# Cross-covariance attention followed by a multiplicative feed-forward layer: an earlier v load, quartered first folds, and a softmax chain issued one operation at a time

## The chip, the core and the metric

The kernel runs on one core of a Trainium2 chip. The core has a matmul engine (TensorE, "PE" in the profile, with its weight loads as "PEld"), a vector engine (VectorE, "DVE"), a scalar engine (ScalarE, "ACT"), a general-purpose engine (GpSimd, "POOL") and a queue engine (SyncE, "SP"). Each runs its own instructions in order and waits for the others by semaphores. Sixteen DMA engines move data for all of them. Matmul results go to PSUM, of which the kernel uses eight banks of 128 x 512 f32; everything else lies in SBUF. The metric is the device time of one execution in microseconds (us), taken as the median of several executions.

## What is computed

```python
def _attn_ref(q, k, v, tau):                                  # q, k, v: (4, 5824, 256)
    qn = q / (np.linalg.norm(q, axis=1, keepdims=True) + 1e-06)
    kn = k / (np.linalg.norm(k, axis=1, keepdims=True) + 1e-06)
    s = kn.transpose(0, 2, 1) @ qn / tau                      # (4, 256, 256)
    s = s - s.max(-1, keepdims=True)
    a = np.exp(s)
    a /= a.sum(-1, keepdims=True) + 1e-09
    return v @ a                                              # (4, 5824, 256)

def _moe_ref(x, w1, w2, w3, w_out):                           # x: (23296, 256)
    a = x @ w1                                                # w1, w2: (256, 1024)
    b = x @ w2
    h = a * b @ w3                                            # w3: (1024, 1024)
    return h @ w_out                                          # w_out: (1024, 256)
```

The attention matrix is only 256 x 256 for each of the four batches, since it is formed over the channels.

## The kernel before

**Algebra.** The attention matrix of a batch is folded into the weights: Wf = softmax x [w1, w2] (256 x 2048 for each batch), so that a and b come straight from v. Likewise W = w3 x w_out (1024 x 256) is formed once. Per batch there remain the scores G = q^T k with the norms of q's and k's columns, the softmax, the fold of w1 and w2, and the main work: a and b for all 5824 rows, their product, and the product times W.

**Main work.** `emit_ab(b, c, j)` (L423) makes one unit: batch b, chunk c of 512 rows (twelve chunks, the last of 192), column block j of eight. Four matmuls of 512 columns give a and b in two PSUM tiles of the tag "ab", which has four buffers; ScalarE casts a to bf16 ("as", L435), and VectorE multiplies it with b ("abs", L444). `emit_out` (L454), two units behind, multiplies the product with W into the PSUM tag "out" (three buffers); after eight units the result is copied by ScalarE and VectorE (L490, L491) and stored by SyncE. A buffer of a is free after its cast, a buffer of b after its product. The tag "G" (one buffer) holds the scores of the next batch.

**Order of the work.** The instructions are placed by hand (`manual_schedule`). While a batch's main work is emitted, `make_agenda(b)` (L604) lists other work for that time with due times, and `run_due` (L385) emits an item once a planned clock has passed its time. The clock counts the planned TensorE time of the emitted matmuls and a cost stated with each item. So an item stands at a place in every engine's queue that its due time sets; it isn't moved at run time.

**The items.** For batch n = b + 1: loads of q, k and v in pieces of eight rows a partition, each issued by GpSimd behind a tiny copy that waits for earlier work (L414 to L421); the 69 score units (`score_units`, L167) spread between t0 and t1; and the softmax (`soft_units`, L239) after t1:
- `norms` (L253): VectorE adds the two halves of the summed squares, and GpSimd sums them over all partitions.
- `k_row` (L262): 1/(sqrt(k's sum) + 1e-6) as four ScalarE operations in place, Ln, Exp, Ln, Exp, one directly behind the other (L271 to L274).
- `q_sums` and `q_norm` (L290, L293): VectorE takes q's sums from the diagonal, ScalarE takes Ln and Exp of them, VectorE adds 1e-6 and inverts.
- `scaled` (L316): two VectorE products of G with k's row (L306), then two ScalarE exponentials with q's factor as scale (L311), all four in one item.
- `sums` (L337): four matmuls with one column for the row sums, in a buffer of the tag "ab", and rs = 1/sum on VectorE.
- eight `fold`s (L359), each of two matmuls of 512 columns: fold i covers half i // 4 of the columns, w1 or w2 by i // 2 % 2, and 128 of the 256 rows by i % 2. Its result is evicted to Wf with the factor rs, by ScalarE for even i and by VectorE for odd i (L355, L357).

**The first batch.** Its scores and squares are matmuls that run as the pieces of q and k arrive (L540 to L578), with warm-up matmuls (`busy`, L205) in between. GpSimd issues the loads in the order of the code: k and q, then w1 and w2 in halves of 512 columns with the two halves of v's first piece between them, more of v, w_out and w3 (L552 to L563). After the scores come `scaled_first` and, behind four more warm-up matmuls, `first_folds` (L366): the row sums, folds 0 to 5, and between folds 2 and 3 eight transposes of v's first half piece on TensorE (`transpose_half_on_pe`, L138), whose copy to SBUF is VectorE's. Folds 6 and 7 are agenda items among the first units.

Of the kernel before, what the change touches and what calls it, by code (L numbers as in the profile page):

```python
# [15 lines left out]
P = 128  # L16
# [8 lines left out]
def kernel(  # L25
# [213 lines left out]
    def soft_units(n):  # L239
# [7 lines left out]
        def scaled_first():  # L247
            scale(0)
            q_norm(st["ss"])
            scale(1)  # L250
            exps()
# [10 lines left out]
        def k_row():  # L262
# [7 lines left out]
            kr = work.tile([P, C], F32, tag="kr", name=f"kr_{n}", bufs=1)  # L270
            nc.scalar.activation(out=kr, in_=src, func=AF.Ln)  # L271
            nc.scalar.activation(out=kr, in_=kr, func=AF.Exp, scale=0.5)
            nc.scalar.activation(out=kr, in_=kr, func=AF.Ln, bias=eps_t)  # L273
            nc.scalar.activation(out=kr, in_=kr, func=AF.Exp, scale=-1.0)  # L274
            st["kr"] = kr
# [14 lines left out]
        def q_sums():  # L290
            q_norm(diagonal(st["tot"][:, 0, :].rearrange("p (c t) -> p c t", t=P)))
# [16 lines left out]
        def exps():  # L308
            e = work.tile([P, CT, C], BF16, tag="e", name=f"e_{n}", bufs=2)
            for ct in range(CT):  # L310
                nc.scalar.activation(  # L311
                    out=e[:, ct, :], in_=st["s"][:, ct, :], func=AF.Exp, scale=st["r"][:, ct : ct + 1]
                )
            st["e"] = e

        def scaled():  # L316
            for ct in range(CT):
                scale(ct)
            exps()

        def sum_mm(c2):
            if c2 == 0:
                st["sum"] = psum.tile([P, 512], F32, tag="out" if n == 0 else "ab", name=f"sum_{n}", bufs=3 if n == 0 else 4)
                Wf[n] = wf_pool.tile([P, CT, 2, F], BF16, tag="Wf", name=f"Wf_{n}")
# [16 lines left out]
        def fold_mm(i, c2, tag="ab", on_act=None):  # L341
            h, rest = divmod(i, 4)
            w, c1 = divmod(rest, 2)
            if c2 == 0:
                st["fold", i] = psum.tile(
                    [P, 512], F32, tag=tag, name=f"fold_{n}_{i}", bufs={"ab": 4, "out": 3}[tag]
                )
            nc.tensor.matmul(  # L348
                st["fold", i], lhsT=st["e"][:, c2, c1 * P : (c1 + 1) * P], rhs=w12[:, c2, w, h * 512 : (h + 1) * 512],
                start=(c2 == 0), stop=(c2 == CT - 1),  # L350
            )
            if c2 == CT - 1:
                dst = Wf[n][:, c1, w, h * 512 : (h + 1) * 512]
                if on_act if on_act is not None else i % 2 == 0:
                    nc.scalar.activation(out=dst, in_=st["fold", i], func=AF.Copy, scale=st["rs"][:, c1 : c1 + 1])  # L355
                else:
                    nc.vector.tensor_scalar_mul(dst, st["fold", i], st["rs"][:, c1 : c1 + 1])  # L357

        def fold(i, tag="ab", on_act=None):  # L359
            fold_mm(i, 0, tag)  # L360
            fold_mm(i, 1, tag, i % 2 == 0 if on_act is None else on_act)

        def first_folds():
            sum_mm(0)
            fold_mm(0, 0)
            fold_mm(1, 0)  # L366
            sum_mm(1)
            fold_mm(0, 1)
            fold_mm(1, 1)
            fold(2)  # L370
            transpose_half_on_pe(0, 0, 0, False)
            fold(3, on_act=True)
            fold(4, "out", on_act=False)
            fold(5, "out")

        if n == 0:
            return [k_first, k_row, q_first, scaled_first, first_folds] + [lambda i=i: fold(i) for i in range(6, 8)]
        head = [(0.0, norms), (0.0, k_row), (0.0, q_sums)]
        return head + [(0.0, scaled), (0.2, sums)] + [(0.43, lambda i=i: fold(i)) for i in range(8)]


# [171 lines left out]
    for h in range(2):  # L553
# [150 lines left out]
```

## Time and profile before

| | |
|---|---|
| time, median of five executions | 574.86 us (574.6 to 576.18) |
| profiled execution, its own time | 574.86 us |
| profiled execution, span | 573.1 us |
| TensorE busy | 559.5 us, 98% of the span |
| TensorE weight loads busy | 355.5 us, 62% |
| VectorE busy | 377.2 us, 66% |
| ScalarE busy | 337.8 us, 59% |
| GpSimd busy | 83.2 us, 15% |
| granted TensorE clock, mean | 0.997 |

The page of the profile gives busy shares, then the span in 40 slices, the DMA queues, the chain of work that ended last, and the costliest groups of instructions. A group's line names line, engine, operation and tiles, the number of instructions, and after the bar the busy time, the mean length and the idle time before them with what ended it. Timelines give the start of a row, its length, and in square brackets the idle time in front of it. A matmul's length includes its way through the array, so rows of one engine overlap, and the busy share of TensorE is not a share of its peak. "Waits" names who waited for whom; where an instruction waits for several things, the one that came last is named.

### The profile page before, as it was taken

What the parts mean: (1) busy time and instruction counts of PE and PEld (TensorE: products, weight loads), DVE (VectorE), ACT (ScalarE), POOL (GpSimd) and SP (SyncE); (2) the same over time, 40 slices, a digit from 0 to 9 for tenths busy, and PEclk for the clock granted to TensorE, in tenths of its full rate; (3) what the DMA queues carried; (4) which work ended last, traced back from release to release, by engine and by line L of the source; (5) the groups of instructions that cost most, each with busy time, mean ns of one, the idle gap of its engine ahead of it and who ended that gap; (6) DMA issues with size and microseconds to landing.
All of it is one profiled execution on the core that took longest, in us unless ns stands there. A gap on an engine that the chain in (4) does not pass through costs nothing.

```text
span 573.1 us, 10096 instructions
## 1 busy us (share of the span) xinstructions
PE 559.5 (98%) x3744; PEld 355.5 (62%) x3750; DVE 377.2 (66%) x612; ACT 337.8 (59%) x624; POOL 83.2 (15%) x164
## 2 busy tenths in 40 slices
PE   7899999999999999999999999999999999999997
PEld 4765576776665666666656666666665666666665
DVE  1047744788877567887776567778876656565564
ACT  0046535777856567776756567767756554454453
POOL 5250020312030111211030012031120000000000
PEclk9899999999999999999999999999999999999999
DMA  8999959779665697395661595665740325221011
GB/s 165 211 189 209 197 99 231 180 160 231 132 174 120 127 204 148 88 195 118 144 147 59 108 218 118 138 138 121 181 110 38 85 73 148 63 62 75 38 70 59
DMA packets 74560, 76.93 MB, mean 134 GB/s; under 512 B 54160, under 2 KB 58256, under 8 KB 74512
## 3 DMA queue, kind: packets, MB, share of 16 engines
q0 software_dynamic: 15504, 39.46, 38.6%
q1 hardware_dynamic: 58784, 36.64, 22.1%
q8 instruction: 29, 0.48, 0.3%
q10 hardware_dynamic: 224, 0.20, 0.1%
q14 instruction: 19, 0.16, 0.1%
HBM read 78.91 MB, written 23.86 MB: 179 GB/s over the span
## 4 chain that ended last, share of the span: by engine, by line
PE 89%; ACT 4%; DMA 3%; DVE 2%; issue 1%; POOL 1%; ACTq 0%; DVEq 0%; POOLq 0%
PE o L470 26%; PE a L429 26%; PE b L429 26%; PE G L188 5%; DMA q<-in_q_dram 3%; PE fold L348 2%; ACT as L435 2%; DVE abs L444 1%; PE G L233 1%; PE w L587 1%; ACT e L311 1%; PE sqq L221 1%; PE sqk L221 0%; POOL k L109 0%; ACT kr L273 0%
## 5 line engine op out<-in xcount | busy, mean ns | idle before, releaser
L444 DVE TENSOR_TENSOR abs<-as,b 128x512 bf16<-128x512 bf16 x336 | 230.0, 686 | 140.9 <-ACT as L435 130.3
L435 ACT CAST as<-a 128x512 bf16<-128x512 f32 (+1 forms) x384 | 215.6, 563 | 178.8 <-DVE abs L444 92.1
L429 PEld LDWEIGHTS <-Wf 128*128 128x128 bf16 x1536 | 149.2, 98 | 102.6 <-issue 2.1
L429 PE MATMUL a<-vT,Wf 128*128 128x512 bf16 x704 | 209.4, 379 | 0.5 <-ACT as L435 0.5
L470 PE MATMUL o<-W_sb,abs 128*128 128x256 bf16 x1376 | 209.5, 273 | 0.1
L429 PE MATMUL b<-vT,Wf 128*128 128x512 bf16 x704 | 209.4, 379 | 0.0
L470 PEld LDWEIGHTS <-abs 128*128 128x128 bf16 x1376 | 134.4, 98 | 81.6 <-DVE abs L446 0.3
L197 DVE TENSOR_TENSOR acc<-acc,sq 128x1024 f32<-128x1024 f32 x66 | 80.5, 1219 | 0.2 <-ACT sq L185 0.2
L188 PE MATMUL G<-k,q 128*128 128x256 bf16 x276 | 49.8, 273 | 0.0
L185 ACT ACTIVATE sq<-q 128x512 f32<-128x512 bf16 x66 | 41.8, 633 | 0.0
L185 ACT ACTIVATE sq<-k 128x512 f32<-128x512 bf16 x66 | 41.6, 630 | 0.0
L417 POOL COPY gate_t<-abs 1x1 bf16<-1x1 bf16 x39 | 13.8, 354 | 170.0 <-DVE abs L444 169.3
L491 DVE COPY osb<-o 128x512 f32<-128x512 f32 x44 | 30.2, 686 | 0.7 <-PE o L470 0.7
L188 PEld LDWEIGHTS <-q 128*128 128x128 bf16 x276 | 27.0, 98 | 3.1
L421 POOL COPY gate_t<-vT 1x1 bf16<-1x1 bf16 x17 | 4.3, 254 | 168.9 <-DMA vT<-v 168.9
L490 ACT COPY osb<-o 128x512 f32<-128x512 f32 x44 | 25.8, 587 | 4.0 <-PE o L470 2.1
L271 ACT ACTIVATE kr<-row 128x256 f32<-128x256 f32 x1 | 0.4, 384 | 31.8 <-PE row L266 31.8
L109 POOL DMA_DIRECT2D q<-in_q_dram x29 | 15.6, 539 | 12.9 <-DMA k<-in_k_dram 5.6
L348 PE MATMUL fold<-w,e 128*128 128x512 bf16 x61 | 16.7, 379 | 0.3
L355 ACT ACTIVATE Wf<-fold,rs 128x512 bf16<-128x512 f32 x16 | 10.9, 687 | 7.9 <-PE fold L348 6.4
L244 DVE TENSOR_TENSOR dk<-sqk,ident 128x256 f32<-128x256 f32 x1 | 0.4, 425 | 21.7 <-PE sqk L221 21.7
L109 POOL DMA_DIRECT2D k<-in_k_dram x25 | 13.7, 548 | 3.7 <-DMA k<-in_k_dram 1.9
(90 smaller groups left out, 241.9 us busy)
## 6 DMA issues: line engine op xcount, KB each, us to landing
out_dram<-osb SPq DMA_DIRECT2D x44, 512.0 KB, 3.1
k<-in_k_dram POOLq DMA_DIRECT2D x19, 512.0 KB, 8.5
v<-in_v_dram POOLq DMA_DIRECT2D x19, 512.0 KB, 5.1
q<-in_q_dram POOLq DMA_DIRECT2D x18, 512.0 KB, 6.6
w_wout<-in_moe_w_dram POOLq DMA_DIRECT2D x1, 2048.0 KB, 23.1
k<-in_k_dram POOLq DMA_DIRECT2D x4, 320.0 KB, 9.9
v<-in_v_dram POOLq DMA_DIRECT2D x4, 320.0 KB, 5.3
q<-in_q_dram POOLq DMA_DIRECT2D x4, 256.0 KB, 11.9
```

What stands on the lines that cost most here:

```text
L109: nc.gpsimd.dma_start(out=pieces[nm, n, pi][:, lo:hi, :], in_=qk_main[nm, n][0][:, pi * PIECE + lo : pi * PIECE + hi, :])
L185: nc.scalar.activation(out=dst[:, :, part, :], in_=src[:, o : o + 2, :], func=AF.Square)
L188: nc.tensor.matmul(G[:, ct, :], lhsT=qt[:, i, ct * P : (ct + 1) * P], rhs=kt[:, i, :], start=(pr == 0 and part == 0 and ct == 0), stop=(pr ...
L197: nc.vector.tensor_add(accs[n], accs[n], sqs[0])
L348: nc.tensor.matmul(st["fold", i], lhsT=st["e"][:, c2, c1 * P : (c1 + 1) * P], rhs=w12[:, c2, w, h * 512 : (h + 1) * 512], start=(c2 == 0), ...
L417: nc.gpsimd.tensor_copy(gate_t, last_ab[0][:1, :1])
L429: nc.tensor.matmul(t[:, :n], lhsT=Wf[b][:, ct, w, j * P : (j + 1) * P], rhs=rhs_of(b, c, ct), start=(ct == 0), stop=(ct == CT - 1),)
L435: nc.scalar.copy(a_sb[:, :n], tiles[0][:, :n])
L444: nc.vector.tensor_mul(ab, a_sb, tiles[1])
L470: nc.tensor.matmul(tl[h][:, o, :], lhsT=lhsT, rhs=W_sb[:, j, :], start=(j == 0 and o == 0), stop=(j == FT - 1 and (small or o == 1)), skip ...
L490: nc.scalar.copy(o[:, 0:2, :], tl[0])
L491: nc.vector.tensor_copy(o[:, 2:4, :], tl[1])
```

## The change

Three things are changed together.

1. The first batch's loads: the first half of v's first piece is loaded ahead of w1 and w2, whose first 512 columns now come in two pieces of 256 each; the second halves of w1 and w2 follow in one piece each. The transposes of v's first half piece move from between the folds to the place between the warm-up matmuls (three instead of four) and the row sums.
2. The first batch's folds: the folds of the first 512 columns are made as eight results of 256 columns, in the order w1, w2, w1, w2; the first four use the tag "ab", the last four the tag "out". The folds of the other 512 columns, four of them, are agenda items among the first units.
3. The softmax of batches 1 to 3: each of the four k operations, q's sums, q's factor, each of the two products with k's row and each of the two exponentials is an agenda item of its own, 0.6 to 2.8 units of the clock apart. The row sums use the tag "G" in place of "ab". The folds are due later (from 18.0 in place of 15.5 after t1 + 1 and t1), 0.85 apart in place of 0.9. In the first batch's agenda t0 and t1 are 56 and 115 in place of 57 and 116.

```diff
@@ soft_units(n)
+        def k_step(i):
+            kr = st["kr"]
+            nc.scalar.activation(
+                out=kr, in_=kr if i else st["row"], func=(AF.Ln, AF.Exp)[i % 2],
+                scale=(1.0, 0.5, 1.0, -1.0)[i], bias=eps_t if i == 2 else 0.0,
+            )
...
         def q_sums():
-            q_norm(diagonal(st["tot"][:, 0, :].rearrange("p (c t) -> p c t", t=P)))
+            st["ss"] = diagonal(st["tot"][:, 0, :].rearrange("p (c t) -> p c t", t=P))
...
-        def scaled():
-            for ct in range(CT):
-                scale(ct)
-            exps()
+        def exps(ct):
+            if ct == 0:
+                st["e"] = work.tile([P, CT, C], BF16, tag="e", name=f"e_{n}", bufs=2)
+            nc.scalar.activation(
+                out=st["e"][:, ct, :], in_=st["s"][:, ct, :], func=AF.Exp, scale=st["r"][:, ct : ct + 1]
+            )
...
-                st["sum"] = psum.tile([P, 512], F32, tag="out" if n == 0 else "ab", name=f"sum_{n}", bufs=3 if n == 0 else 4)
+                st["sum"] = psum.tile([P, 512], F32, tag="out" if n == 0 else "G", name=f"sum_{n}", bufs=3 if n == 0 else 1)
...
         def first_folds():
             sum_mm(0)
-            fold_mm(0, 0)
-            fold_mm(1, 0)
+            for c1 in range(CT):
+                fold_mm((0, c1, 0, 256), 0)
             sum_mm(1)
-            fold_mm(0, 1)
-            fold_mm(1, 1)
-            fold(2)
-            transpose_half_on_pe(0, 0, 0, False)
-            fold(3, on_act=True)
-            fold(4, "out", on_act=False)
-            fold(5, "out")
+            for c1 in range(CT):
+                fold_mm((0, c1, 0, 256), 1, on_act=c1 == 0)
+            for w, lo in ((1, 0), (0, 256), (1, 256)):
+                for c1 in range(CT):
+                    for c2 in range(CT):
+                        fold_mm((w, c1, lo, lo + 256), c2, "ab" if lo == 0 else "out", c1 == 0)
 
         if n == 0:
-            return [k_first, k_row, q_first, scaled_first, first_folds] + [lambda i=i: fold(i) for i in range(6, 8)]
-        head = [(0.0, norms), (0.0, k_row), (0.0, q_sums)]
-        return head + [(0.0, scaled), (0.2, sums)] + [(0.43, lambda i=i: fold(i)) for i in range(8)]
+            return [k_first, k_row, q_first, scaled_first, first_folds] + [lambda i=i: fold(i) for i in range(4, 8)]
+
+        return (
+            [(0.0, 0.0, norms), (0.0, 7.5, k_row)]
+            + [(0.0, 7.5 + 1.3 * i, lambda i=i: k_step(i)) for i in range(4)]
+            + [(0.0, 8.0, q_sums), (0.0, 10.8, lambda: q_norm(st["ss"]))]
+            + [(0.0, 13.0 + 1.3 * ct, lambda ct=ct: scale(ct)) for ct in range(CT)]
+            + [(0.0, 13.6 + 1.3 * ct, lambda ct=ct: exps(ct)) for ct in range(CT)]
+            + [(0.2, 17.0, sums)]
+            + [(0.43, 18.0 + 0.85 * i, lambda i=i: fold(i)) for i in range(8)]
+        )
@@ loads and order of the first batch
-    for h in range(2):
-        hs = slice(h * F // 2, (h + 1) * F // 2)
-        nc.gpsimd.dma_start(out=w12[:, :, 0, hs], in_=w1r[:, :, hs])
-        nc.gpsimd.dma_start(out=w12[:, :, 1, hs], in_=w2r[:, :, hs])
-        if h == 0:
-            new_piece("v", 0, 0)
-        load_part("v", 0, 0, h * half, (h + 1) * half)
+    new_piece("v", 0, 0)
+    load_part("v", 0, 0, 0, half)
+    for f0, f1 in ((0, 256), (256, 512), (512, F)):
+        nc.gpsimd.dma_start(out=w12[:, :, 0, f0:f1], in_=w1r[:, :, f0:f1])
+        nc.gpsimd.dma_start(out=w12[:, :, 1, f0:f1], in_=w2r[:, :, f0:f1])
+    load_part("v", 0, 0, half, PIECE)
...
     soft0[3]()
-    busy(4)
+    busy(3)
+    transpose_half_on_pe(0, 0, 0, False)
     soft0[4]()
@@ make_agenda(b)
-            for i in range(2):
-                at(1.5 + 0.6 * i, 0.43, soft0[5 + i])
+            for i in range(4):
+                at(0.8 + 0.6 * i, 0.43, soft0[5 + i])
...
-            t0, t1 = 57.0, 116.0
+            t0, t1 = 56.0, 115.0
...
-        late = 2.5 if b == 0 else 0.0
-        ts = [t1 + 1.0] + [t1 + late + t for t in (8.5, 9.0, 11.0, 14.5)] + [t1 + late + 15.5 + 0.9 * i for i in range(8)]
-        for t, (cst, fn) in zip(ts, soft):
-            at(t, cst, fn)
+        for i, (cst, t, fn) in enumerate(soft):
+            at(t1 + 1.0 + t + (2.0 if b == 0 and i > 0 else 0.0), cst, fn)
```

## The prediction

> **What bounds the kernel now.** I read the page's chain first, then the waits of TensorE, then the timelines of single engines where TensorE stops, then the transfers of the first 45 us. The chain that ended last:
>
> ```profile
> PE 89%; ACT 4%; DMA 3%; DVE 2%; issue 1%; POOL 1%; ACTq 0%; DVEq 0%; POOLq 0%
> ```
>
> TensorE sets the time: a microsecond is won only where it stops, and its matmul work is the same before and after (64 fold matmuls, eight of them cut in two; one 0.22 us warm-up less, which lies in idle time). It stops at two kinds of place that the change touches. The first is the turn from scores to the first chunk (timeline of TensorE, then of ScalarE; columns are start, length, engine, line, operation, idle before it):
>
> ```profile
> 34.95 1.03 PE L209 MATMUL warm_I-482_483<-warm 128*128 128x512 bf16 x3
> 36.98 0.20 PE L327 MATMUL sum<-ones_b,e 128*128 128x1 bf16 x2 [1.00 <-ACT e L311]
> ...
> 37.53 1.02 PE L348 MATMUL fold<-w,e 128*128 128x512 bf16 x4
> 38.39 0.61 PE L132 MATMUL tr_I-511_512<-ident_b,v 128*128 128x128 bf16 x8
> 38.83 1.46 PE L348 MATMUL fold<-w,e 128*128 128x512 bf16 x6
> 40.13 0.59 PE L429 MATMUL a<-vT,Wf 128*128 128x512 bf16 x2
> ```
> ```profile
> 36.42 0.91 ACT L311 ACTIVATE e<-s,r 128x256 bf16<-128x256 f32 x2 [0.44 <-DVE r L298]
> 38.16 2.00 ACT L355 ACTIVATE Wf<-fold,rs 128x512 bf16<-128x512 f32 x3 [0.83 <-PE fold L348]
> ```
>
> TensorE waits for e until 36.98 and then runs without a gap to the first a at 40.13: 3.15 us, 0.44 of it (38.39 to 38.83) the transposes of v. Matmuls are spaced 0.217 us (512 columns), 0.109 (256), 0.083 (192) and 0.055 (128); a row's length adds a pipeline tail. The second kind of place is the softmax of a later batch. Batch 3, TensorE, then ScalarE:
>
> ```profile
> 434.45 0.60 PE L470 MATMUL o<-W_sb,abs 128*128 128x256 bf16 x4
> 435.87 0.24 PE L327 MATMUL sum<-ones_b,e 128*128 128x1 bf16 x4 [0.82 <-ACT as L435]
> 436.36 0.59 PE L429 MATMUL a<-vT,Wf 128*128 128x512 bf16 x2 [0.25 <-ACT as L435]
> ```
> ```profile
> 432.54 0.60 ACT L490 COPY osb<-o 128x512 f32<-128x512 f32 x1
> 434.44 0.91 ACT L311 ACTIVATE e<-s,r 128x256 bf16<-128x256 f32 x2 [1.31 <-DVE s L306]
> 435.25 1.05 ACT L435 CAST as<-a 128x512 bf16<-128x512 f32 x2
> ```
>
> The reader should see that ScalarE sits 1.31 us in front of its exponentials and that two casts lie behind them; "sum" takes one of the four a/b buffers and so waits for the first of those casts, not for e (ready at 435.35). By spacing, TensorE loses 435.87-434.45-0.44 = 0.98 and 436.36-435.87-0.10 = 0.39: 1.37 us. Batch 2 shows the same steps at 300.46, 301.88 and 302.37: 1.37. Batch 1 stops at the last chunk's start:
>
> ```profile
> 172.45 0.60 PE L470 MATMUL o<-W_sb,abs 128*128 128x256 bf16 x4
> 173.28 0.32 PE L429 MATMUL a<-vTt,Wf 128*128 128x192 bf16 x2 [0.23 <-ACT as L435]
> 173.76 0.33 PE L429 MATMUL b<-vTt,Wf 128*128 128x192 bf16 x2 [0.16 <-ACT as L435]
> 174.00 0.61 PE L470 MATMUL o<-W_sb,abs 128*128 128x256 bf16 x4
> ```
>
> That is 0.39+0.31+0.08 = 0.78, and further on gaps of 0.03 to 0.30 before folds and a/b of the short chunk (174.5 to 182.3), 0.9 in all.
>
> **The change, part by part.**
>
> *First stage, loads.* Each answer below is for one issue, at 29.85, 31.64 and 32.18 us in this order; the last column is microseconds to landing:
>
> ```profile
> w<-in_moe_w_dram POOLq DMA_DIRECT2D x1, 256.0 KB, 4.6
> v<-in_v_dram POOLq DMA_DIRECT2D x1, 256.0 KB, 5.6
> w<-in_moe_w_dram POOLq DMA_DIRECT2D x1, 256.0 KB, 7.0
> ```
>
> The last one lands at 39.18, where a weight load for fold 4 indeed waits for w until 39.18. v's first half now takes the place of the first w1 piece, so it lands near 34.5 (29.85+4.6); its eight transposes, placed behind three warm-up matmuls (34.95+0.65 = 35.6), run in the wait for e: -0.44 on the path. Their copy on VectorE (0.69, L136) fits between the second scale (ends 36.70) and rs (37.70). The w pieces follow: neighbours of 256 KB landed 1.2 to 1.9 us apart (34.45, then 30.56+5.2 = 35.76, 37.24, 39.18), so a quarter of 128 KB costs at least 0.6 and, if a piece cost the same whatever its size, at most 1.9; I take 0.9, because rows of half the length lower the rate (163 GB/s at 550 packets in 30 to 32 us, 219 at 123 packets in 20 to 22). The fourth quarter then lands at 34.6+3.6 = 38.2; TensorE reaches it at 38.6. The halves land near 39.7 and 41.1, wanted at 40.6 and 42.4; v's second half and piece 1 about 42.5 and 45.3, wanted at 44.2 and 47. GpSimd issues two DMAs more (0.72 each); behind them w3 is issued later, but it landed 23.1 us after issue, so the transfers are its limit, and its transposes (landed 63.1) had 3.4 us before the first w matmul at 66.50.
>
> Behind these spacings stands a rule that speaks against small pieces: the Trainium skill (DMA: Bandwidth & Descriptors, "Anatomy of one DMA — SWDGE (gpsimd) path") gives a DMA about 2.0 us fixed plus the bytes at 436 GB/s, which as an estimate makes 2.3 us a quarter; paid one after another, the fourth would land at 43.8 and the sum be some 5 us worse. Pieces of twice the size landing 1.2 to 1.9 us apart say that it is not paid in series.
>
> *First stage, folds.* In the built program's order folds 0 to 3 stand ahead of the first a as eight 256-column quarters, and folds 4 to 7 between the first a/b units (before: 0 to 5 ahead, 6 and 7 between). Four quarters use the "ab" buffers and four the three "out" buffers, so the eighth waits until ScalarE has evicted the fifth, and behind it the whole of TensorE's queue. ScalarE starts evicting at 38.16 (rs as before) and takes the first, third and fifth quarter in turn; a 128x256 ScalarE instruction with a scale vector costs 0.455 (e: 0.91 for two): the fifth is out at 38.16+3x0.455 = 39.53. TensorE is at the eighth by 38.83 (second sum at 37.47 as before, then 12 more matmuls), so it waits 0.7, ends it at 39.75 and has 2x0.433 = 0.87 us of folds more to come than before at 40.13. Net 39.75+0.87-40.13 = +0.49, say **+0.45**. From below: no wait, only the moved transposes, -0.44. From above: late pieces (rival D), +3.4.
>
> *Scores of batch 1.* With t0 at 56 and two folds more behind the first a, the score units stand up to 1.3 us earlier in TensorE's work; the first matmul on piece 4 of k 0.44 earlier. That one had little room: k's piece, issued at 128.01, landed after 10.2 at 138.2; its first G matmul started at 138.63. The gates in front of the load stand where they stood. 0 to +0.8, nearest to **+0.15**.
>
> *Softmax of batches 1 to 3.* The four kr steps, 0.42 to 0.51 each, now go singly between casts, before each of which ScalarE idled 0.71: they cost nothing as long as that idle time stands (else 0.4 a step). "sum" takes the G buffer, free once the second scale has read it, so it no longer takes an a/b buffer or waits for a cast. What stays is a round trip: in batches 2 and 3 the order is cast, product, scale, exponential, next cast. One round is 0.60+0.42+0.47+0.59 = 2.1 against 1.30 for a unit of TensorE; two rounds put ScalarE 1.6 behind, and a cast may lag about 1.3 (a's buffer is wanted again 2.17 after a ends; the cast itself takes 0.59, its start 0.2). A stall of about 0.35 is left, in front of a of the unit 10_7: -1.0 per batch. In exchange five or six folds move from full units, where they ran without gaps, into the short chunk, where batch 1 lost 0.9 with seven: +0.3 each, bounds 0 and 0.9. In batch 1 each exponential stands a cast later than its scale, so no round trip: -0.78; its folds start two units later, three at the end together: -0.2, bounds -0.9 and 0. Sum -1.0-0.7-0.7 = **-2.4**; bounds -4.4 (all stops gone: 0.78+0.9+2x1.37) and +1.5 (no slack in the rounds, 1.6+0.9-1.37 in two batches, -0.78 in the first).
>
> Casts between Ln and Exp cost no switch of tables: in the block of batch 3 a cast follows Exp at 435.25 with no idle time. The skill (ScalarE: Activation LUTs, "Table sets: the hidden batching unit") asks that calls be grouped by table set; at its 2.7 us a switch, a switch at every one of the eight split operations would make the sum some 20 us worse a batch.
>
> **Sum.** +0.45+0.15-2.4 = -1.8. The profiled execution took 574.86 us (span 573.1, 1.76 around it), the median itself, so 574.86-1.8 = 573.06: **573.1 us**.
>
> **Rivals.** B: the round trip eats batches 2 and 3; only batch 1 gains: 574.86+0.6-1.0 = 574.5. For it: the 1.31 us that ScalarE waits for scales today; against it: the buffers' slack. C: ScalarE evicts 256 columns in 0.37 (L480's copy) or the eighth quarter isn't held: start 0 to -0.44, 572.2. D, the other side: quarters land 1.9 us apart. The fourth is there at 42.2, 3.6 late, 0.7 of it covered: start +0.45+2.9, and the halves behind it another 0.7; 574.86+4.05+0.15-2.4 = 576.7. It passes the old time from about 1.45 us a quarter and the bound of what can be told from 1.75. Against it: two of the three spacings above are under 1.5 at twice the bytes. E, the change doesn't do what it says: v's half lands only at 37.24 as today, the transposes hold up the sums until 37.7: +0.7, 573.8.
>
> **How the numbers follow.** Likeliest case 0.60 (571.9 to 573.9: start -0.1 to +1, softmax -3 to -1.5), B 0.15, C 0.12, D 0.08, E 0.05. The range 571.9 to 575.2 leaves out D and the lower part of C. About 0.2% (1.15 us) is what can be told from no change. Faster, below 573.7: 0.54 of the likeliest, C, part of E: 0.67. Slower, above 576.0: D and a little: 0.09. Between: 0.24.
>
> **What would show it.** The v transposes in TensorE's timeline before the sums; the eighth quarter waiting for ScalarE near 38.8 to 39.5 and the first a near 39.7; no wait of "sum" on a cast, but one of some 0.3 of a on a cast in batches 2 and 3. Wrong if TensorE waits for w or v before 45 us, for k near 138 us, or if the short chunks lose more than 0.9 each.

## The result and the profile after

| | before | after |
|---|---|---|
| median | 574.97 us (62 executions, 574.6 to 576.72) | 575.71 us (36 executions, 573.95 to 579.84) |
| ratio | | 1.002, 95% interval 1.0012 to 1.0029 |
| profiled execution, its own time | 574.86 us | 574.51 us |
| profiled execution, span | 573.1 us | 572.4 us |

So the kernel became slower by 0.2%, where 573.1 us was forecast. The scatter says more than the median: before, all executions lie within 2.1 us, after they reach over 5.9 us, and thirteen of the 36 lie above 577. (Beside runs 9 to 12 two of 23 executions of the kernel before took 577.45 and 580.08 us: a single high execution shows nothing, thirteen of 36 do.) The one that was profiled took 574.51, 0.35 us less than the profiled one before. It still shows what went wrong. The chain of work that ended last, by engine and by line:

```profile
PE 85%; DMA 12%; POOL 1%; issue 1%; DVE 1%; ACT 1%; POOLq 0%; ACTq 0%; DVEq 0%
PE a L440 26%; PE b L440 26%; PE o L481 25%; DMA k<-in_k_dram 8%; PE G L188 4%; PE fold L350 2%; DMA v<-in_v_dram 2%; PE w L598 1%; DMA w<-in_moe_w_dram 1%; DMA vT<-v 1%; ACT as L446 0%; POOL q L109 0%; POOL k L109 0%; DVE abs L455 0%; POOL w L568 0%
```

DMA stood at 3% and is now at 12%, 8% of it loads of k. TensorE's timeline shows the place (start, length, engine, line, operation, idle before it with its releaser):

```profile
116.79 0.38 PE L188 MATMUL G<-k,q 128*128 128x256 bf16 x2 [0.20 <-DMA k<-in_k_dram]
...
137.64 0.60 PE L481 MATMUL o<-W_sb,abs 128*128 128x256 bf16 x4
139.19 0.60 PE L188 MATMUL G<-k,q 128*128 128x256 bf16 x4 [0.95 <-DMA k<-in_k_dram]
```

The brackets count idle time only; by spacing of the matmuls (139.19-137.64-0.44 = 1.11, and 0.36 at 116.79) TensorE loses **1.47 us** in front of scores of batch 1, because pieces 2 and 4 of k come late. Before, it lost nothing there:

```profile
138.19 0.60 PE L470 MATMUL o<-W_sb,abs 128*128 128x256 bf16 x4
138.63 0.60 PE L188 MATMUL G<-k,q 128*128 128x256 bf16 x4
```

The other two places changed in the way that was planned, the start at a higher cost. The start, TensorE:

```profile
35.24 0.61 PE L132 MATMUL tr_I-491_492<-ident_b,v 128*128 128x128 bf16 x8
36.62 0.20 PE L328 MATMUL sum<-ones_b,e 128*128 128x1 bf16 x2 [0.77 <-ACT e L318]
...
39.19 0.59 PE L440 MATMUL a<-vT,Wf 128*128 128x512 bf16 x2
...
40.44 0.59 PE L350 MATMUL fold<-w,e 128*128 128x512 bf16 x2 [0.23 <-DMA w<-in_moe_w_dram]
```

The transposes of v run in the wait for e, and the first a stands 2.57 us behind the first sum (before 3.15); with two folds more still to come, the fifth unit of a and b begins 8.66 us behind the sum (45.28-36.62), before 7.91 (44.89-36.98): +0.75 at equal work. And the softmax of batch 3:

```profile
438.19 0.60 PE L481 MATMUL o<-W_sb,abs 128*128 128x256 bf16 x4
438.62 0.24 PE L328 MATMUL sum<-ones_b,e 128*128 128x1 bf16 x4
438.88 0.59 PE L440 MATMUL a<-vT,Wf 128*128 128x512 bf16 x2
```

"sum" follows o without a wait (0.98 before); 0.16 and 0.06 are left in front of a and b, and some tenths between the folds that follow.

The account of the two profiled executions closes: the first sum 0.36 us earlier (in the execution before, the granted clock was one half from 21.20 to 24.61 us, among the scores of batch 0, and in this one it was not; for loads this one waited 0.5 us longer), start +0.75, k +1.47, and from the fifth unit to the last matmul 523.36 instead of 524.41, that is -1.05 with the 1.47 in it, so -2.52 for the softmax of three batches. Together -0.66; the spans differ by -0.67. (The time around the span was 2.1 instead of 1.8 us; why isn't known.)

**Why k is late.** GpSimd's timeline, before and then after: one-element copies to gate_t are the gates, which wait for the work named behind the arrow, and the DMA_DIRECT2D rows are the issues of loads.

```profile
72.22 0.18 POOL L421 COPY gate_t<-vT 1x1 bf16<-1x1 bf16 x1 [34.71 <-DMA vT<-v]
...
81.84 0.18 POOL L421 COPY gate_t<-vT 1x1 bf16<-1x1 bf16 x1 [8.25 <-DMA vT<-v]
...
126.76 0.18 POOL L421 COPY gate_t<-vTt 1x1 bf16<-1x1 bf16 x1 [13.97 <-DVE acc L197]
128.01 0.54 POOL L109 DMA_DIRECT2D k<-in_k_dram  x1
```
```profile
73.79 0.18 POOL L432 COPY gate_t<-vT 1x1 bf16<-1x1 bf16 x1 [34.72 <-DMA vT<-v]
...
85.01 0.18 POOL L432 COPY gate_t<-vT 1x1 bf16<-1x1 bf16 x1 [9.86 <-DMA vT<-v]
...
127.56 1.04 POOL L432 COPY gate_t<-vTt 1x1 bf16<-1x1 bf16 x1 [14.79 <-DVE abs L455]
129.67 0.54 POOL L109 DMA_DIRECT2D k<-in_k_dram  x1
```

Read downwards this is one chain: a transpose of v by SyncE's DMA lands, the gate opens, the next piece of v is loaded, is transposed, opens the next gate, behind which q and k are loaded, and so on. It begins with w3: SyncE transposes w3 in four steps ahead of v's third piece, and w3 landed at 60.41 instead of 59.14 (issue 37.57 with 22.8 us to landing; before 36.03 with 23.1). So the first gate opens 1.57 us later, the second 3.17, the last 0.80. In front of the last one the piece of v is issued when it was before (111.68, before 111.71), but lands 0.79 us later, behind the loads of q and k that the gates made late. The bracket of the last gate names VectorE; the transpose that it reads landed at 127.43 (before 126.64), 0.13 us (0.12) ahead of the copy, so it is this landing that opens the gate. There the copy itself takes 1.04 instead of 0.18, and the k load that lands at 139.14 is issued 1.66 us later than its counterpart, which landed at 138.19. TensorE wanted it at 138.63 before and at 138.08 now. The slow copy coincides with a sum of squares on VectorE, which before had just ended (before, then after):

```profile
125.44 1.22 DVE L197 TENSOR_TENSOR acc<-acc,sq 128x1024 f32<-128x1024 f32 x1
```
```profile
127.34 1.22 DVE L197 TENSOR_TENSOR acc<-acc,sq 128x1024 f32<-128x1024 f32 x1
```

The copy of 127.56 ends 0.04 us after this sum. So of the 1.66 us, 0.80 is the chain and 0.86 what the gate met by being late.

w3 itself is late because the loads ahead of it took longer (v's second half landed at 42.97, before at 41.69). Two windows of the first stage, before and then after (length, busy time of the engines with counts, granted clock, share of the DMA engines, GB/s):

```profile
35.50:37.50 2.00, 0.99 (x7) 0.29 (x6) 0.99 (x4) 1.35 (x5) 1.86 (x3) 1.00 1.03 168
```
```profile
35.50:37.50 2.00, 1.23 (x17) 0.79 (x15) 1.61 (x7) 1.03 (x3) 2.00 (x4) 1.00 0.97 127
```

The DMA engines are about as busy as before, but move 127 instead of 168 GB/s. A quarter's rows are 512 bytes, those of a half 1024, those of v 2048; the window before holds 163 packets of 1024 bytes and 83 of 2048, the one after 227 of 512 and 134 of 1024, so the order of the loads has its share in the difference. With the same order and halves (run 6 below) the window holds 302 packets of 1024 and none of the others:

```profile
35.50:37.50 2.00, 0.81 (x13) 0.40 (x10) 1.88 (x5) 1.08 (x3) 1.86 (x3) 1.00 1.10 155
```

A packet of 512 bytes took 61 ns in the mean of 28 to 60 us, one of 1024 between 104 and 108. By these times the quarters cost the sixteen engines 0.75 us more, of the 1.27 by which w3 is late; the rest is not accounted for.

The second gate lost more than the first, since the transposes in front of it took 5.3 us to land instead of 3.6. From the transfers while they run, before (78 to 82 us) and then after (79.5 to 85 us): an issue with its microseconds to landing, and a queue with its packets, MB and share of the engines:

```profile
vT<-v SPq DMA_TRANSPOSE x1, 3.6
```
```profile
q8 instruction: 1, 0.02, 1.1%
...
vT<-v SPq DMA_TRANSPOSE x1, 5.3
```

The transposes move 2080 packets in both; but after, one instruction fetch of 16 KB falls before the landing. In the packets of the trace all but two of the transposes' have started by 82.88; the fetch runs from 82.90 to 83.86, and the last two follow at 83.84 and 83.85. Before, the last ones moved at 81.25 and the fetch came at 83.16.

### The profile page after: what moved, and what is told of

It reads as the page before. It is cut to its first block, busy times and chain, and to the rows that moved or that the text cites. A ratio compares the mean times of both kernels' runs of the same rounds, so it can differ in the third digit from the quotient of the medians.

```text
span 572.4 us, 10114 instructions
## 1 busy us (share of the span) xinstructions
PE 558.8 (98%) x3751; PEld 355.1 (62%) x3757; DVE 377.3 (66%) x614; ACT 337.6 (59%) x626; POOL 85.8 (15%) x166
## 4 chain that ended last, share of the span: by engine, by line
PE 85%; DMA 12%; POOL 1%; issue 1%; DVE 1%; ACT 1%; POOLq 0%; ACTq 0%; DVEq 0%
PE a L440 26%; PE b L440 26%; PE o L481 25%; DMA k<-in_k_dram 8%; PE G L188 4%; PE fold L350 2%; DMA v<-in_v_dram 2%; PE w L598 1%; DMA w<-in_moe_w_dram 1%; DMA vT<-v 1%; ACT as L446 0%; POOL q L109 0%; POOL k L109 0%; DVE abs L455 0%; POOL w L568 0%
## 5 line engine op out<-in xcount | busy, mean ns | idle before, releaser
L197 DVE TENSOR_TENSOR acc<-acc,sq 128x1024 f32<-128x1024 f32 x66 | 80.5, 1219 | 0.7 <-ACT sq L185 0.7
L350 PE MATMUL fold<-w,e 128*128 128x512 bf16 (+1 forms) x69 | 16.6, 354 | 1.3 <-ACT Wf L357 0.6
L357 ACT ACTIVATE Wf<-fold,rs 128x512 bf16<-128x512 f32 (+1 forms) x18 | 11.3, 640 | 7.7 <-PE fold L350 7.3
## 6 DMA issues: line engine op xcount, KB each, us to landing
w_wout<-in_moe_w_dram POOLq DMA_DIRECT2D x1, 2048.0 KB, 22.8
```

Of the source, the lines that this page charges most:

```text
L197: nc.vector.tensor_add(accs[n], accs[n], sqs[0])
L350: nc.tensor.matmul(m, lhsT=st["e"][:, c2, c1 * P : (c1 + 1) * P], rhs=w12[:, c2, w, lo:hi], start=(c2 == 0), stop=(c2 == CT - 1),)
```

## The experiments

Three explanations stood at the start: K (k comes late), F (the first stage loses by late w or v) and S (the split softmax does). The first four runs split the change.

**1. Scores at their old place.**

```diff
-            t0, t1 = 56.0, 115.0
+            t0, t1 = 57.0, 116.0
```

> The changed kernel with t0 and t1 of the first batch back at 57 and 116; nothing else. Theory K (k comes late): in the profile of the changed kernel TensorE waits 0.36 us at 116.79 and 1.11 us at 139.19 for pieces of k, because w3's load lands at 60.41 (before: 59.14) and everything queued behind it, down to the k load issued at 129.67 (before: 128.01), is later, while the scores stand about 1 us earlier. With the scores about 0.9 to 1.0 us later the two waits shrink to about 0.1 to 0.3 in all, the profile shows that, the median falls by 1.2 to about 574.5, and the executions of 577 to 580 become rare. Theory F (the first stage makes the slow executions, by w or v coming late): no change, 575.7, with a third of the executions still above 577. Theory S (the split softmax does): no change either.

Measured: 576.4 us (574.08 to 579.53, 12 executions), ratio 1.0025 (1.0009 to 1.0041). The wait did not shrink, it grew:

```profile
141.20 0.38 PE L188 MATMUL G<-k,q 128*128 128x256 bf16 x2 [3.48 <-DMA k<-in_k_dram]
```

This k load was issued at 129.49, as in the changed kernel (129.67), but landed at 141.16 instead of 139.14; a store of the output was issued at 131.78 beside it, in the changed kernel only at 133.35. So theory K is right about the wait and wrong about its cure: one unit of the clock is less than the scatter of that load, which landed at 139.14, 140.76 (run 12) and 141.16 in the three profiles with this first stage and the split softmax.

**2. The split softmax alone.** Loads, folds and transposes of batch 0 as before, t0 and t1 at 57 and 116; of the change only the new agenda of `soft_units` and the row sums in "G". Against the changed kernel:

```diff
-    new_piece("v", 0, 0)
-    load_part("v", 0, 0, 0, half)
-    for f0, f1 in ((0, 256), (256, 512), (512, F)):
+    for h in range(2):
+        hs = slice(h * F // 2, (h + 1) * F // 2)
...
-    busy(3)
-    transpose_half_on_pe(0, 0, 0, False)
+    busy(4)
     soft0[4]()
...
-            t0, t1 = 56.0, 115.0
+            t0, t1 = 57.0, 116.0
```

> The split softmax alone: loads, folds and transposes of the first batch as before, t0 and t1 at 57 and 116. Theory K: no wait for k, and the softmax gains what the trace of the changed kernel shows when its waits are taken out (about 1.2 in batch 1 and 0.67 in each of batches 2 and 3, 2.5 in all): 574.97 - 2.5 = 572.5, executions close together as those of the kernel before. Theory F: the same 572.5. Theory S (the split softmax makes the spread, and gains little): 575 to 576, with executions above 577.

Measured: 573.6 us (573.53 to 573.86), ratio 0.9973 (0.9962 to 0.9983). No wait for k, and no scatter: theory S falls. The gain is 1.5, not 2.5: the last three chunks of a batch take 30.59, 29.90 and 29.74 us here (before 30.87, 30.78, 30.23), which is -0.28 in batch 1 and -0.88 and -0.49 in the others; 0.33 is lost again in the first stage, 0.32 of it to a wait for w at 39.68. In batch 1 the gain does not hang on t1 alone: in run 1, also with t1 at 116, the three chunks took 29.54 us, a gain of 1.1 at equal work (two matmuls of the scores, 0.22 us, lie ahead of them there). The planned clock of run 1 counts two folds more among the first units, 0.86 in all, and so emits what follows earlier; no run changed that alone.

**3. The first stage alone.** The changed kernel's loads, quarter folds and transposes, the old softmax, t0 and t1 at 57 and 116. Against the changed kernel:

```diff
+        def scaled():
+            for ct in range(CT):
+                scale(ct)
+            for ct in range(CT):
+                exps(ct)
...
+        head = [(0.0, norms), (0.0, whole_row), (0.0, whole_q)]
+        return head + [(0.0, scaled), (0.2, sums)] + [(0.43, lambda i=i: fold(i)) for i in range(8)]
...
-            t0, t1 = 56.0, 115.0
+            t0, t1 = 57.0, 116.0
```

> The first stage alone: v's half piece first, w1 and w2 in six loads, quarter folds, transposes ahead of the row sums; the softmax in its old form and t0 and t1 at 57 and 116. Theory K: the stage's own cost is the 0.75 us that the changed kernel is behind at equal work at 45 us, counted from the row sums, and the late k load costs 0.1 to 0.5 more with the scores at their old place: 574.97 + 0.75 + 0.3 = 576.0, few executions above 577.5. Theory F: it holds all of the loss and the spread: 575.7 + 2.5 = 578, a third of the executions above 579. Theory S: 575.0 to 575.7, close together.

Measured: 581.8 us (577.07 to 582.27), ratio 1.0091 (1.0063 to 1.0118). Far above what K expected, and not for w or v either. TensorE, and then a window of it:

```profile
141.18 0.59 PE L188 MATMUL G<-k,q 128*128 128x256 bf16 x2 [2.94 <-DMA k<-in_k_dram]
141.56 1.06 PE L447 MATMUL a<-vT,Wf 128*128 128x512 bf16 x2
```
```profile
142.00:146.00 4.00, 4.00 (x23) 2.37 (x22) 2.35 (x3) 2.26 (x5) 0.00 (x0) 0.77 1.02 200
```

Behind a wait of 3.10 us by spacing the matmuls stand 0.43 us apart instead of 0.216 until 143.9 (two of them take 1.06 instead of 0.59): the granted clock is one half, 0.77 in the mean of the window, its column behind the counts. From 141.18 on that costs 1.3 us more. Of its 6.5 us over the span before, 0.64 is the start, 3.26 the waits for k (0.16 of it at 118) and 1.3 the clock; the other 1.3 lie mostly in the old softmax of batch 1, which the folds moved behind the first unit put at another place (next run).

**4. The kernel before with early scores.**

```diff
-            t0, t1 = 57.0, 116.0
+            t0, t1 = 56.0, 115.0
```

> The kernel before with t0 and t1 at 56 and 115; nothing else. Theory K: the k piece that lands at 138.19 had 0.44 us to spare; with the scores about 1 us earlier TensorE waits some 0.5 us for it: 575.4 to 575.6, and the profile shows the wait near 138. It lacks the late w3, so its executions scatter less than those of the changed kernel. Theories F and S: 575.0, no wait for k.

Measured: 577.2 us (576.84 to 577.77), ratio 1.0035 (1.0023 to 1.0047), above what any theory gave. The wait for k is there as expected (0.56 by spacing, at 138.15). The larger part is another: with the earlier t1 the old softmax falls into full chunks.

```profile
171.48 0.59 PE L429 MATMUL a<-vT,Wf 128*128 128x512 bf16 x2 [0.22 <-ACT as L435]
...
173.95 0.59 PE L429 MATMUL a<-vT,Wf 128*128 128x512 bf16 x2 [0.71 <-ACT as L435]
```

With a b between them, TensorE loses 0.38, 0.29 and 0.88 by spacing. So the shift of t1 is bad for the old softmax; the split one, in the changed kernel, does not lose by it.

What the four leave: k is late wherever the new first stage is in, with either softmax and either place of the scores. The next four move loads only, to tell theory W (the loads' chain behind a late w3) from rival P (the place of the scores decides, whatever the loads do).

**5. w3 ahead of v's third piece**, in the changed kernel:

```diff
-    load_piece("v", 0, 2)
     nc.gpsimd.dma_start(out=wout_sb, in_=moe_w_out.rearrange("(lh ll) c -> ll lh c", ll=P))
     nc.gpsimd.dma_start(out=w3_bf, in_=w3r)
+    load_piece("v", 0, 2)
```

> The changed kernel with one load moved: v's third piece (512 KB) is issued behind w_out and w3 instead of ahead of them, so w3 lands about 2.4 us earlier, near 58.0. Theory W (the loads' chain): the transposes of w3, those of v, the gates of GpSimd behind them and the loads of q and k behind the gates stand in one chain, and a late w3 makes the k piece late; then the whole chain is earlier by 2 to 3 us, the waits for k near 117 and 139 (1.5 us in the profile of the changed kernel) shrink below 0.6, no execution is above 576.5, and the median is 573.4 to 574.2. Rival P (the place of the scores decides, whatever the loads do): 575.7 with the same scatter, as when t0 and t1 were put back.

Measured: **573.11 us** (572.74 to 573.72, five executions), ratio 0.9962 (0.995 to 0.9974). w3 landed at 59.20 (58.0 was expected), the second gate's transposes took 3.7 us from 78.92, k was issued at 127.87 and landed at 137.85, just in time (no bracket, so no wait; in the chain that ended last DMA is at 6%):

```profile
137.89 0.60 PE L188 MATMUL G<-k,q 128*128 128x256 bf16 x4
```

One moved load takes 2.6 us from the median and the scatter with it, at the same place of the scores: rival P falls.

**6. w1 and w2 in halves**, in the changed kernel:

```diff
-    for f0, f1 in ((0, 256), (256, 512), (512, F)):
+    for f0, f1 in ((0, 512), (512, F)):
```

> The changed kernel with w1 and w2 loaded in halves of 512 columns (four loads in place of six; v's half piece still first, quarter folds unchanged). Theory W: the 256-column loads have rows of 512 bytes and made everything behind them 1.3 us late (v's second half landed at 42.97, before 41.69; w3 at 60.41, before 59.14); with halves w3 is back near 59.1, the wait for k falls to about 0.5 (as in the kernel before with early scores: 0.56), the executions above 577 vanish, the median is 574.0 to 574.7. The folds wait no more than 0.3 for w at 37 to 38. Rival P: 575.7, same scatter.

Measured: 573.31 us (573.09 to 575.98; ten of twelve below 573.6), ratio 0.9971 (0.9962 to 0.998). w3 landed at 59.52, k at 137.95, and TensorE lost 0.20 by spacing for it. The folds don't miss the quarter loads: the start to the fifth unit takes 8.26 us behind the sum instead of 8.66 (in run 12, with quarters, 8.26 too).

**7. Quarter loads alone**, added to the kernel of run 2: everything else of the first stage old.

```diff
-    for h in range(2):
-        hs = slice(h * F // 2, (h + 1) * F // 2)
+    for f0, f1 in ((0, 256), (256, 512), (512, F)):
```

> The kernel with the split softmax alone (573.6, executions within 0.3 us) with one thing added: the first 512 columns of w1 and w2 are loaded in quarters of 256; order, folds and the rest stay. Theory W: w3 lands 1 to 1.3 us later, the transposes of v's fourth piece meet the instruction fetch at 82 to 83 us and take 5.3 instead of 3.6 us, the q and k loads of batch 1 come up to 3 us later, TensorE waits 1 to 3 us for k near 139: median 575 to 577, executions spread over 3 us. Rival P: 573.6 to 574.0, close together.

Measured: 574.8 us (573.86 to 575.43), ratio 0.9991 (0.9982 to 1.0): 1.2 us worse than run 2, but not where theory W put it.

```profile
PE fold L350 <- DMA w<-in_moe_w_dram: 0.6, 1, 0.6
PE tr_I-513_514 L132 <- DMA v<-in_v_dram: 0.6, 1, 0.6
```

v's half piece and the third pair of w pieces came late to TensorE itself (0.75 and 0.78 by spacing). w3 landed at 60.90 as expected; but with TensorE later too (the fifth unit at 46.59, in run 2 at 45.32), the fetch came at 84.35, behind the transposes (80.03 to 83.70, 3.7 us), and k, landed at 140.27, was waited for nowhere. Here the late w3 cost nothing at k, and TensorE had lost its 1.2 us already in the first stage.

**8. A candidate:** run 2 with v's half piece loaded first and transposed ahead of the row sums, w in halves, folds of 512 columns, and v's third piece behind w3. Against run 2:

```diff
-    for h in range(2):
+    new_piece("v", 0, 0)
+    load_part("v", 0, 0, 0, half)
+    for f0, f1 in ((0, 512), (512, F)):
...
-    busy(4)
+    busy(3)
+    transpose_half_on_pe(0, 0, 0, False)
     soft0[4]()
...
-    load_piece("v", 0, 2)
     nc.gpsimd.dma_start(out=wout_sb, in_=moe_w_out.rearrange("(lh ll) c -> ll lh c", ll=P))
     nc.gpsimd.dma_start(out=w3_bf, in_=w3r)
+    load_piece("v", 0, 2)
```

> A candidate: the split softmax, t0 and t1 at 57 and 116, v's half piece loaded first and transposed ahead of the row sums, w1 and w2 in halves and folds of 512 columns as before, v's third piece behind w3. Theory W: no wait for k; the transposes leave the path (-0.44) and a wait for the third pair of w pieces of 0.3 stays: 573.6 - 0.4 = 573.2, close together. Rival P: 573.6 or more, since the place of the scores moves with the stage.

Measured: 572.96 us (572.76 to 573.56), ratio 0.9962 (0.995 to 0.9974), as expected; a wait of 0.35 by spacing for k is left, which was not.

The last four ask for the dose, and for an execution of the changed kernel that is slower than the first.

**9 and 10. w3 late by itself.** In the kernel of run 2, loads of 128 KB ahead of w_out (two in run 9, four in run 10), whose data nothing reads:

```diff
+    for i in range(2):
+        nc.gpsimd.dma_start(out=W_sb[:, 2 * i : 2 * i + 2, :], in_=w1r[:, :, i * 256 : (i + 1) * 256])
     nc.gpsimd.dma_start(out=wout_sb, in_=moe_w_out.rearrange("(lh ll) c -> ll lh c", ll=P))
```

> The kernel with the split softmax alone (573.6; first stage, scores and folds as before) with two loads added ahead of w_out and w3: 128 KB each, of w1's columns again, into space that W takes later. They are work for nothing; no other load of the first stage is touched. Theory W, if it holds without any change of the first stage: w3 lands 1.4 us later, near 61.0, the transposes of v's fourth piece run from about 80.3 and meet the instruction fetch at 83.0, so they take 5.3 instead of 3.7 us; TensorE waits 1 to 3 us for k near 139; median 574.6 to 576.5, spread over 2 us. If the transposes escape the fetch, as with the quarter loads: no wait for k, 573.6 to 574.0. Rival Q (only the first stage of the changed kernel makes k late, through the order of its folds): 573.6.

> The same with four such loads: w3 near 62.4, the transposes of v's fourth piece from 81.7, the fetch in the middle of them. Theory W: k 2 to 4 us late, with the half clock after it in some executions: median 576 to 578.5, more than with two loads. Rival Q: 573.6.

Measured: with two 575.82 us (574.47 to 578.53), ratio 1.0013 (0.9997 to 1.0029); with four 578.44 us (576.36 to 579.35), ratio 1.0049 (1.0032 to 1.0067). From 573.6 that is +2.2 and +4.8. The transposes took 5.3 and 5.7 us, and TensorE lost 0.88 and 3.06 us by spacing for k. The longest wait with four:

```profile
142.73 0.49 PE L188 MATMUL G<-k,q 128*128 128x256 bf16 x3 [2.66 <-DMA k<-in_k_dram]
```

With four, TensorE waited another 0.56 us for the transposed w3 itself, at 71.01. The order of the first stage's folds and transposes isn't touched (the fifth unit starts 8.44 and 8.48 us behind the sum, in run 2 8.24), and the time and the scatter of the changed kernel appear: theory W holds, rival Q falls. The profile with two is of an execution of 574.63; the slower ones were not profiled.

**11. Halves and w3 ahead at once**, in the changed kernel (the edits of runs 5 and 6).

> A candidate: the changed kernel with w1 and w2 in halves and with v's third piece behind w3, both at once. Theory W: no wait for k; against 573.11 with w3 ahead alone, the wait of 0.56 us for w at 40.55 goes too, against 573.31 with halves alone the wait of 0.20 for k: 572.6 to 573.0.

Measured: 573.02 us (572.81 to 573.62), ratio 0.9961 (0.9948 to 0.9974). No wait for k. It is not below run 8 by more than the scatter; both beat the kernel before by 0.4%.

**12. The changed kernel again.**

> The changed kernel once more, beside the kernels above. Theory W: 575 to 576.5 with executions from 574 to 580; in its profile the wait for k near 139 is as long as the time is high (574.5 went with 1.1 us; 577 to 578.5 would go with 3 us or more and a granted clock of one half for about 3.4 us). Rival Q and all others: the same time, but a slow execution would show its loss elsewhere.

Measured: 576.06 us (574.55 to 580.31, 12 executions), ratio 1.0022 (0.9998 to 1.0046). The profiled execution took 576.1 us, and TensorE:

```profile
117.73 0.38 PE L188 MATMUL G<-k,q 128*128 128x256 bf16 x2 [1.42 <-DMA k<-in_k_dram]
...
140.80 0.60 PE L188 MATMUL G<-k,q 128*128 128x256 bf16 x4 [1.62 <-DMA k<-in_k_dram]
```

1.59 and 1.79 by spacing, 3.38 in all, where the execution of 574.51 lost 1.47. That is 1.91 more for 1.59 us more of time; the start to the fifth unit was 0.40 shorter (no wait for w at 40). So these two executions differ by the wait for k, and run 5, which takes the wait away, takes the scatter too. Executions above 577 were not caught by a profile in this kernel; that they add the half clock of run 3 is likely and not shown (their mean granted clock is 0.996 or 0.997 but for one, that of the others mostly 0.998 to 1.0; but the profiled execution before has 0.997 too, from its half clock at 21.20, and took 574.86).

All kernels in one table; the waits by spacing, from one profiled execution each:

| kernel | w3 landed | v's transposes before the second gate: start, us to landing | k issued, landed | wait for k | median |
|---|---|---|---|---|---|
| before | 59.14 | 78.08, 3.6 | 128.01, 138.19 | 0 | 575.0 |
| after | 60.41 | 79.61, 5.3 | 129.67, 139.14 | 1.47 | 575.7 |
| after, again | 60.51 | 80.16, 5.8 | 130.60, 140.76 | 3.38 | 576.1 |
| 1 late scores | 60.55 | 80.38, 5.4 | 129.49, 141.16 | 3.65 | 576.4 |
| 3 first stage | 61.34 | 80.91, 5.4 | 129.96, 141.13 | 3.26 | 581.8 |
| 9 two loads more | 61.47 | 80.61, 5.3 | 130.17, 139.84 | 0.88 | 575.8 |
| 10 four loads more | 62.38 | 82.40, 5.7 | 131.49, 142.69 | 3.06 | 578.4 |
| 7 quarter loads | 60.90 | 80.03, 3.7 | 129.85, 140.27 | 0 | 574.8 |
| 4 early scores | 60.02 | 79.28, 3.6 | 128.34, 138.10 | 0.56 | 577.2 |
| 2 softmax alone | 59.62 | 78.95, 3.7 | 128.40, 138.84 | 0 | 573.6 |
| 5 w3 ahead | 59.20 | 78.92, 3.7 | 127.87, 137.85 | 0.07 | 573.1 |
| 6 halves | 59.52 | 78.94, 3.7 | 127.88, 137.95 | 0.20 | 573.3 |
| 11 both | 56.86 | 76.68, 3.6 | 127.58, 137.40 | 0 | 573.0 |
| 8 candidate | 56.55 | 76.26, 3.6 | 127.84, 138.38 | 0.35 | 573.0 |

With the old loads w3 landed at 59.14, 59.62 and 60.02 (before, runs 2 and 4), with the loads of the changed kernel at 60.41 to 61.34 (after, runs 12, 1 and 3). Where it landed by 60.02 the wait for k is at most 0.56; where it landed later the wait is 0.88 or more, but for run 7. The size of the wait doesn't follow w3's landing alone.

## Why the prediction was wrong

- **The step that failed is "Scores of batch 1"**, taken at +0.15 with bounds 0 and +0.8. It measured +1.47 in the execution of 574.51 us and +3.38 in that of 576.1. The earlier scores alone, with the old loads, cost 0.56 in run 4, within the bounds; what lies beyond is the late load. With the wait taken away by run 5 the kernel stands at 573.11 us, where the prediction stood; that it is so close is luck in part: in its profile the start costs 0.92 instead of 0.45 (0.56 of it a wait for w at 40.55), and the first sum comes 0.43 us early, which no term of the prediction holds.
- **What it rested on** is a cover in the step on the loads: w3 is issued later, "but it landed 23.1 us after issue, so the transfers are its limit, and its transposes had 3.4 us before the first w matmul". The transfers are indeed the limit; but with the quarters they got 1.3 us slower themselves, and the 3.4 us are the room of w3's first reader only. On SyncE's queue the transposes of v stand behind those of w3, and GpSimd's gates and loads behind those: that row of waiters was never walked. "The gates in front of the load stand where they stood" is true of their place in the order and not of their time, since a gate opens when a DMA lands.
- The prediction saw that the k piece had only 0.44 us of room (138.63 against 138.19), and named "for k near 138 us" among the things that would prove it wrong. It priced the earlier scores against that room, and not a later load.
- **First stage, folds: +0.45; measured +0.75** in the first profile and +0.35 in run 12 (8.26 against 7.91). The mechanism holds. In run 6 the eighth quarter waits 0.58 by spacing for ScalarE instead of 0.7, which starts evictions of 256 columns 0.35 to 0.38 us apart instead of 0.455; in the first profile 0.57 is lost there too, 0.32 at the seventh quarter for the fourth piece of w (landed at 38.45) and 0.25 at the eighth for ScalarE. The 0.40 that the first profile lost beyond run 12 was for the halves of w, landed at 40.40 instead of the 39.7 that was worked out and wanted at 40.04 instead of 40.6.
- **First stage, loads.** The quarters landed 0.68, 0.72, 0.66 and then 1.97 us apart (35.10, 35.82, 36.48, 38.45 behind v's 34.42), within the bounds of 0.6 and 1.9 but for the last; the mean is 1.0 for the 0.9 taken. The rule of the Trainium skill (DMA: Bandwidth & Descriptors, "Anatomy of one DMA — SWDGE (gpsimd) path") of about 2.0 us for each was, as argued, not paid in series. The sum of the whole train of loads, +1.3 at its end, was worked out as far as v's piece and not carried on to w3.
- **Softmax: -2.4; measured -2.52** (-1.15, -0.88, -0.49 for -1.0, -0.7, -0.7). Right, "sum" in "G" included. Not seen: the -1.15 in batch 1, counted at equal work, does not come with the split by itself: in run 2 it is -0.28, in run 1, also with t1 at 116, -1.1.
- **Rivals.** D (late w quarters) is in part what run 7 shows, in another kernel; it isn't what happened. Of C the premise came true (evictions 0.35 to 0.38 us apart), but not what it gave: the eighth quarter was held, and the start did not gain. B and E did not happen. The slower side was given 0.09 with D alone as its mechanism; a second one stood in the text as a term of the sum, with a bound taken from today's slack alone.

## What to carry to other kernels

When a change delays a load, walk its whole row of waiters: not only the first reader of the data, but what stands behind it on that queue, and what gates those open. A gate fixed in the order of instructions isn't fixed in time if what it waits for is a DMA. And a median that hardly moves while the scatter triples was here the sign that a slack had been used up: look for a new wait in the profile of any execution, even a quick one, and take that before judging the rest of the change.

## What the runs showed of the hardware

- **An instruction fetch among DMA transposes.** In eight of the fourteen profiles the fetch of 16 KB at 81 to 85 us starts with the last packets of the transposes in front of the second gate, or behind them, and they land 3.6 to 3.7 us after issue; in six it starts while packets are still to come, and they land after 5.3 to 5.8. The order of the packets in the changed kernel (the last two held until the fetch ends) speaks for it as the cause; no kernel moved the fetch alone. The lateness of k doesn't need it either: in run 7 k was issued at 129.85 and landed at 140.27 without it.
- **Half a clock behind a stall.** In run 3 the granted clock fell to one half at 140.5, 2.4 us into a stall, and stayed there for 3.41 us. In run 1 a longer stall (3.65) left it at 1.00. In the kernel before it fell at 21.20, 0.8 us after a wait of 2.43 us for q had ended, again for 3.41 us. The Trainium skill (TensorE: Matmul & The Clock Gate, Part 1) describes a free-running window of about 3.4 us by whose activity the clock is set; the length agrees with the 3.41 us here, and a window that need not begin with the stall would let a stall of 3.65 us pass and would bring the half clock after a shorter one.
- **Short rows.** A DMA packet of 512 bytes took 61 ns where one of 1024 took 104 to 108 (28 to 60 us, before and after): 8.4 against 9.5 to 9.8 bytes a nanosecond.
- **GpSimd's gate** of one element takes 0.18 us or up to 1.26 (1.04 at 127.56 in the changed kernel, 0.93 in run 12). In the fourteen profiles 176 of these copies took over 0.3 us; each of them began with or during VectorE's sum `acc<-acc,sq` (L197: two f32 inputs, 1.22 us) and ended 0.04 us after it. Of the 213 that began beside VectorE's product of two bf16 inputs (`abs`) and not beside the sum, 211 took 0.18, one 0.27, and one, which began with the next sum, 1.26. So a copy that meets the f32 sum is held until the sum ends. It is no part of what makes k late in runs 1, 3 and 10, where the last gate took 0.18 us and k landed at 141.13 to 142.69.
